# All of w_in decoded ahead of the mish part and parked in DRAM, GpSimd's sums on VectorE, the first token tile in the static order, one DMA a group

## The chip, the cores and the metric

The kernel runs on one core of a Trainium2 chip. The metric is the device time of one execution in microseconds (us). The trace is that of one profiled execution; its views count microseconds from the start of its span.

## What is computed

The reference chains three parts. Landmark attention on q, k and v of 4 batches, 8 heads, 576 positions and 64 columns a head gives x of 2304 tokens by 512. A gated MLP follows, and a mish MLP:

```python
def _moe_ref(x, w1, w2, w3, w_out) -> np.ndarray:
    a = x @ w1
    b = x @ w2
    h = a * b @ w3
    return (h @ w_out).astype(np.float32)
...
def _moe2_ref(x, w_in, w_out) -> np.ndarray:
    h = x @ w_in
    sp = np.where(h > 20.0, h, np.log1p(np.exp(np.minimum(h, 20.0))))
    g = h * np.tanh(sp)
    return (g @ w_out).astype(np.float32)
```

The mish MLP is 512 to 2048 to 512 wide, and is what the change is about. Its weights arrive as 64-bit words and are decoded to fp32 on the core.

## The kernel before, in words

Every product is made of three matmuls on split operands: `mm3` (L197 to L200) multiplies high by high, high by low and low by high part. "Hi" is a rounded copy (`copy`, on ScalarE L227, on GpSimd L229), "lo" what is left over (`less`, L232).

**Stages.** The attention and the weight products come first. Then, for each pair of batches, the products a and b (`xa`, `xb`), whose product `xm` goes to a tile `h`, and the y stage, which multiplies `h` with the combined weight W3: eight units u (half a batch each), of four blocks `y u m` of 24 matmuls each. A unit needs `h` split into hi and lo first: eight `sh u k` on ScalarE and eight `sl u k` on VectorE, into one of two `hs` buffers, so the split of unit u+1 waits until unit u-1 has been multiplied. The y stage of units 2 to 7 is the last before the mish part.

**The mish part.** It works on three token tiles of 768 tokens, and for each tile on eight groups (q = 0 to 7) of 256 columns of w_in: 24 groups g. A group's product with w_in is done by a seven-product scheme on 2x2 blocks: PE makes `Z0` to `Z6` (six matmuls of 384 columns each, lines L198 to L200 with `zw` or `hs` as weights) in two PSUM banks, and the banks are read between them. In order of a group: ScalarE copies bank 0 (`S`, L1310), VectorE makes `Q` (L1313), ScalarE mish (`E1`, two activations, L1272 and L1273), VectorE `R` (L1322), the sums `C22` and `C21` (L1332, L1333), mish `E2`, sum `C12` (L1339), mish `E3`, and the lo parts `L1`, `L2`, `L3` (L232). Z6 writes bank 0 again and must wait until C22 has read it; Z0 of the next group waits in the same way for C12, and Z4 for E1. Between them PE does the output products of the group before, in four parts `O0` to `O3` of nine matmuls of 512 columns (`o_part`). Group 0 has no such parts.

**What feeds it.** w_in and w_out of this part come in 32 units n of 512 KB (`x_ops`): load `ld n` on SP's queue into one of four raw buffers, `da` (ScalarE L210), `dm` (VectorE L216), `ds` (ScalarE L219), `db` (VectorE L223). w_in units go to `wf`, 512 columns at a time. For w_out unit f follow `wh f` (ScalarE), `wl f` (GpSimd, L232) and `ws f`, a store of the split unit to DRAM, as later tiles load it again. For each quad q of w_in columns GpSimd makes four sums `zs0` to `zs3` (L1037), seven `zh` (ScalarE) and seven `zl` (VectorE) split the operands into a `zw` buffer (two of them, 14 KB a partition), and `zd q` stores them to DRAM. Tokens are treated alike: four sums `yt` (GpSimd, L1037), seven `yh` and seven `yl` for each token tile.

**The order.** Each engine works its instructions off in the order in which the program issues them. Up to the y stage's end this is the list `ORDER`, written out token by token. In it stand the loads and decoding of units 0 to 3 and 8 to 11 (the first 1024 columns of w_in) and 4 to 7, quads 0 and 1, and the token operands of tile 0. For groups 0 to 7 a second list, `WITH`, says after which of the group's steps the rest is issued: units 12 to 31, quads 2 to 7. From group 6 on a `zw` buffer's seven parts of 256 KB are loaded from DRAM, each right behind the product that frees it (`after_z`, L1303), and two split w_out units of 512 KB a group (L1347). SP's queue carries all these loads and stores and is worked off in order too. In the last group of a tile the seven `yh` and `yl` of the next tile stand right behind the products that free their buffers.

Of the kernel before, what the change touches and what calls it, by code (L numbers as in the profile page):

```python
# [1396 lines left out]
```

## Time and profile before

| | us |
|---|---|
| median of 3 runs | 775.21 (774.81 to 776.62) |
| the profiled execution's own time | 775.96 |
| its span, first to last instruction | 774.18 |
| busy: PE, VectorE (DVE), ScalarE (ACT), GpSimd (POOL) | 739.4, 454.2, 346.0, 158.6 |

The span is what the trace covers; 1.78 us of the profiled execution's time lie outside it. Matmuls are pipelined, and a busy PE is not PE at its peak.

### The profile page before, as it was taken

How to read it: one execution, taken by the hardware profiler on the slowest of the kernel's cores; microseconds unless marked ns; L12 is line 12 of the kernel's file. 1: busy time of each engine (PE TensorE's matmuls, PEld its weight loads, DVE VectorE, ACT ScalarE, POOL GpSimd, SP SyncE). 2: the span in 40 equal slices, each digit the busy share in tenths (PEclk: the TensorE clock that was granted, in tenths of full speed). 3: DMA queues.
4: the chain of work that ended last, by engine and by line, in shares of the span. 5: the costliest groups of instructions: out<-in, count | busy, mean ns of one | idle time of the engine just before them, and what ended most of it. 6: DMA issues, size and time to landing. Idle time of an engine off the chain costs nothing.

```text
span 774.2 us, 13579 instructions
## 1 busy us (share of the span) xinstructions
PE 739.4 (96%) x5236; PEld 623.0 (80%) x5236; DVE 454.2 (59%) x870; ACT 346.0 (45%) x753; POOL 158.6 (20%) x176
## 2 busy tenths in 40 slices
...
GB/s 323 374 269 74 152 135 248 148 84 138 55 164 136 145 48 85 174 1 150 109 239 251 273 208 233 346 230 208 222 181 166 175 193 240 206 177 166 175 1 82
DMA packets 61440, 135.16 MB, mean 175 GB/s; under 512 B 5312, under 2 KB 22080, under 8 KB 60352
## 3 DMA queue, kind: packets, MB, share of 16 engines
...
q8 instruction: 41, 0.67, 0.4%
...
## 4 chain that ended last, share of the span: by engine, by line
PE 79%; DMA 7%; DVE 6%; ACT 4%; issue 2%; POOL 0%; SPq 0%; ACTq 0%; POOLq 0%; DVEq 0%
PE ps L198 23%; PE ps L200 23%; PE ps L199 23%; PE ps L363 4%; DMA raw<-in_w3T_dram 3%; DMA raw<-in_wo_dram 3%; PE ps L854 2%; DVE raw L216 2%; DMA raw<-in_w_dram 1%; PE ps L653 1%; DMA raw<-in_wi_dram 1%; ACT W L1273 1%; PE ps L457 1%; DVE yH L232 1%; ACT raw L219 1%
## 5 line engine op out<-in xcount | busy, mean ns | idle before, releaser
L198 PE MATMUL ps<-hs,W 128*128 128x288 f32 (+1 forms) x298 | 92.7, 311 | 0.0
L199 PE MATMUL ps<-hs,W 128*128 128x288 f32 (+1 forms) x298 | 92.1, 309 | 0.0
L200 PE MATMUL ps<-hs,W 128*128 128x288 f32 (+1 forms) x298 | 92.1, 309 | 0.0
L1272 ACT ACTIVATE hsb<-hsb 128x768 f32<-128x768 f32 (+1 forms) x48 | 32.9, 686 | 124.3 <-DVE hsb L1333 87.6
L216 DVE TENSOR_SCALAR raw<-raw 128x512 uint16<-128x512 uint16 x88 | 72.8, 862 | 24.7 <-ACT raw L210 24.4
L198 PE MATMUL ps<-AT,M 128*128 128x288 f32 x256 | 79.0, 309 | 1.7 <-ACT a L227 1.6
L199 PE MATMUL ps<-AT,M 128*128 128x288 f32 x256 | 75.5, 295 | 0.0
L200 PE MATMUL ps<-AT,M 128*128 128x288 f32 x256 | 75.5, 295 | 0.0
L363 PE MATMUL ps<-wo,raw 128*128 128x512 f32 x128 | 65.6, 639 | 7.8 <-DVE raw L223 5.9
L219 ACT ACTIVATE raw<-raw 128x512 f32<-128x512 f32 x88 | 58.7, 676 | 25.6 <-DVE raw L216 25.6
L210 ACT ACTIVATE raw<-raw 128x512 int32<-128x512 uint16 x72 | 48.3, 673 | 43.3 <-DMA raw<-in_w3T_dram 14.9
L198 PEld LDWEIGHTS ps<-hs,W 128*128 128x128 f32 x298 | 56.2, 188 | 3.0 <-issue 0.8
L200 PEld LDWEIGHTS ps<-hs,W 128*128 128x128 f32 x298 | 56.3, 189 | 1.7
L199 PEld LDWEIGHTS ps<-hs,W 128*128 128x128 f32 x298 | 56.5, 190 | 1.5
L198 PEld LDWEIGHTS ps<-AT,M 128*128 128x128 f32 x256 | 48.0, 188 | 11.5 <-ACT a L227 2.8
L232 DVE TENSOR_TENSOR W<-hsb,W 128x384 fp32r<-128x384 f32 (+1 forms) x72 | 53.4, 744 | 5.2 <-ACT W L1273 4.8
L363 PEld LDWEIGHTS ps<-wo,raw 128*128 128x128 f32 x128 | 23.6, 204 | 30.7 <-issue 17.2
L199 PEld LDWEIGHTS ps<-AT,M 128*128 128x128 f32 x256 | 48.1, 188 | 0.0
L200 PEld LDWEIGHTS ps<-AT,M 128*128 128x128 f32 x256 | 48.1, 188 | 0.0
L227 ACT ACTIVATE a<-ps 128x288 f32<-128x288 f32 x64 | 26.2, 411 | 39.3 <-PE ps L200 36.9
L1322 DVE TENSOR_TENSOR zt<-ps,zt 128x384 f32<-128x384 f32 x24 | 13.4, 559 | 51.5 <-PE ps L200 51.5
L892 DVE TENSOR_TENSOR h<-a,ps 128x288 f32<-128x288 f32 x64 | 28.4, 452 | 21.4 <-PE ps L200 18.0
...
## 6 DMA issues: line engine op xcount, KB each, us to landing
raw<-in_w_dram SPq DMA_DIRECT2D x64, 256.0 KB, 3.8
zw<-zd SPq DMA_DIRECT2D x56, 256.0 KB, 3.0
hs<-zd SPq DMA_DIRECT2D x56, 256.0 KB, 3.1
...
zd<-zw SPq DMA_DIRECT2D x4, 1792.0 KB, 6.6
zd<-hs SPq DMA_DIRECT2D x4, 1792.0 KB, 6.7
```

Of the source, the lines that this page charges most:

```text
L198: T.matmul(out=o, lhsT=lh, rhs=rh, start=first, stop=False, skip_group_check=partial)
L199: T.matmul(out=o, lhsT=lh, rhs=rl, start=False, stop=False, skip_group_check=partial)
L200: T.matmul(out=o, lhsT=ll, rhs=rh, start=False, stop=last, skip_group_check=partial)
L210: S.activation(w[..., 0], q[..., 1], ACTF.Copy, scale=2.0 ** -13, bias=2.0 ** -14 - 0.5)
L216: V.tensor_scalar(q[..., 1], q[..., 3], 0x8000, None, op0=ALU.bitwise_and)
L219: S.activation(f32(w[..., 1]), f32(w[..., 1]), ACTF.Copy, scale=2.0 ** -112)
L227: S.activation(o, x, ACTF.Copy)
L232: (G if e == "POOL" else V).tensor_tensor(o, x, f32(hi), op=ALU.subtract)
L363: T.matmul(out=got(f"acc{i}"), lhsT=f32(got(f"w3{n}")[:, o:o + 128, 0]), rhs=WO0[j // 4][:, j % 4], start=j == 0, stop=j == 7)
L854: T.matmul(out=got(f"p{c}{key}")[32 * i:32 * i + 32, 0:256], lhsT=LT[r, b, 2 * c + par, :], rhs=w12(f"w{bp}{s}{c}")[r, par * 256:par * 256 ...
L892: V.tensor_tensor(hslice(u, s), got("s" + key), got("b" + key)[:, 0:HALF], op=ALU.mult)
L1272: S.activation(e, src_, ACTF.Mish)
```

## The change

All eight units of columns 1024 to 2047 of w_in (16 to 19, 24 to 27) are decoded first, where units 0 to 3 and 8 to 11 stood, and stored to DRAM as decoded (`wfs 2`, `wfs 3`, 1 MB each); `wfl 2` and `wfl 3` load them when quads 4 and 6 come up. Units 0 to 3 and 8 to 11 move into the end of the ab stage and the y stage, units 12 to 15 and the beginning of 20 into the y stage. Four split w_out units that are ready before their place is free (`STAGED`: f = 1, 2, 3, 5) go to other tiles first, are stored from there, and come back by `wr f`. The sums `zs` and `yt` and the lo parts `wl` are made by VectorE. Groups 0 to 7 are now steps of `ORDER` like the rest; `WITH` is gone. From tile 1 on, one DMA of 1792 KB reloads a `zw` buffer at the end of a group (`reload`), and the next tile's `yt`, `yh`, `yl` stand behind `Q`, `L1`, `E2` and `L3`. The matmuls, the mish steps and their order on PE stay.

```diff
-WITH = (
-    "zs0 2,zs1 2,zs2 2,wh 2,wl 2,da 16|zh0 2,zl0 2,dm 16,ld 18,ws 2|zh1 2,zl1 2,ds 16,wh 3,wl 3,ld 19,ws 3,da 17|zh2 2,zl2 2,db 16,dm 17|zh3 2,zl3 2,zs3 2,ds 17,db 17,da 18,dm 18|zh4 2,zl4 2,zh5 2,zl5 2,zh6 2,zl6 2,zd 2",
...
-MADE = (0, 1, 2, 3, 8, 9, 10, 11, 4, 5, 6, 7, 16, 17, 18, 19, 12, 13, 14, 15, 24, 25, 26, 27, 20, 21, 22, 23, 28, 29, 30, 31)
+MADE = (16, 17, 18, 19, 24, 25, 26, 27, 0, 1, 2, 3, 8, 9, 10, 11, 4, 12, 5, 6, 7, 13, 14, 15, 20, 21, 22, 23, 28, 29, 30, 31)
+STAGED = {1: 0, 2: 1, 3: 2, 5: 3}
...
+    "ds 13,wh 2,db 13,y 7 0,wh 3,wr 1,wl 2,zh0 1,yl6 0,ws 2,ld 15,zh1 1,zh2 1,zh3 1,wl 3,zh4 1,zl0 1,zh5 1,ws 3,"
+    "wh 5,zl1 1,zl2 1,y 7 1,da 14,zl3 1,zl4 1,zl5 1,yh0 0,wl 5,ws 5,yl0 0,da 15,ld 20,y 7 2,zs3 1,dm 14,zh6 1,"
+    "dm 15,ye 7 1,ye 7 0,ye 6 3,zl6 1,ds 14,zd 1,zs0 2,wfl 2,ds 15,zs1 2,db 14,y 7 3,ye 7 2,yh2 0,zs2 2,ld 21,"
+    "da 20,yl2 0,db 15,wr 2,wr 3,dm 20,ye 7 3,wr 5,yt4 1,wh 6,Z0 0,ds 20,wl 6,S 0,Z1 0,db 20,ws 6,ld 22,zh0 2,"
+    "da 21,Q 0,Z2 0,zh1 2,yt1 1,E1 0,Z3 0,zl0 2,zh2 2,R 0,Z4 0,zh3 2,L1 0,Z5 0,C22 0,zh4 2,zl1 2,C21 0,Z6 0,zh5 2,"
+    "zl2 2,E2 0,C12 0,zl3 2,Z0 1,E3 0,L2 0,Z1 1,S 1,L3 0,da 22,Q 1,O0 0,dm 21,yt3 1,ds 21,zl4 2,Z2 1,zl5 2,zs3 2,"
...
+    def zw_all(g):
+        if g % 2:
+            return hs_a()[:, 0:3584]
+        if "zwa" not in LATE:
+            LATE["zwa"] = LATE["pw"].tile([128, 3584], F32R, tag="zw0", name="zw0")
+        return LATE["zwa"]
-        return (hs_a() if g % 2 else HS[2])[:, p * 512:(p + 1) * 512]
+        return zw_all(g)[:, p * 512:(p + 1) * 512]
...
+    def w_made(j):
+        if j == 2:
+            return HS[2][:, 0:2048].rearrange("p (k n) -> p k n", k=4)
+        return wf(j) if j < 2 else HS[3]
+    def w_flat(x):
+        return x.rearrange("p k n -> p (k n)")
+    def w_stage(f):
+        i = STAGED[f]
+        return late(f"W{i // 2}", 2048, f"wst{i // 2}")[:, i % 2 * 1024:(i % 2 + 1) * 1024]
...
-            return ops + [(f"db {n}", "DVE", lambda e: join(r(), wf(j)[:, i]))]
+            return ops + [(f"db {n}", "DVE", lambda e: join(r(), w_made(j)[:, i]))]
+        def to():
+            return w_stage(f) if f in STAGED else wo_slot(f)
         return ops + [
             (f"db {n}", "DVE", lambda e: join(r())),
-            (f"wh {f}", "ACT", lambda e: copy(e, wo_slot(f)[:, 0:512], f32(r()[..., 0]))),
-            (f"wl {f}", "POOL", lambda e: less(e, wo_slot(f)[:, 512:1024], f32(r()[..., 0]), wo_slot(f)[:, 0:512])),
-            (f"ws {f}", "SP", lambda e: nc.sync.dma_start(out=wod[f], in_=f32(wo_slot(f))))]
+            (f"wh {f}", "ACT", lambda e: copy(e, to()[:, 0:512], f32(r()[..., 0]))),
+            (f"wl {f}", "DVE", lambda e: less(e, to()[:, 512:1024], f32(r()[..., 0]), to()[:, 0:512])),
+            (f"ws {f}", "SP", lambda e: nc.sync.dma_start(out=wod[f], in_=f32(to())))]
+    def wo_load(u):
+        nc.sync.dma_start(out=f32(wo_slot(u)), in_=wod[u % (2 * NQ)])
...
-        return [(f"zs0 {q}", "POOL", f(0, a21, a22, ALU.add)),
...
+        return [(f"zs0 {q}", "DVE", f(0, a21, a22, ALU.add)),
+                (f"zs1 {q}", "DVE", f(1, 0, a11, ALU.subtract)),
+                (f"zs2 {q}", "DVE", f(a21, a11, a21, ALU.subtract)),
+                (f"zs3 {q}", "DVE", f(1, a12, 1, ALU.subtract))]
...
-        return [(f"yt4 {t}", "POOL", sub_(y_cuts(t, 0, 1), t_(0), b_(0, 1), b_(0, 0))),
...
+        return [(f"yt4 {t}", "DVE", sub_(y_cuts(t, 0, 1), t_(0), b_(0, 1), b_(0, 0))),
...
+                (f"yt5 {t}", "DVE", sub_(y_cuts(t, 0), t_(1), b_(1, 0), t_(1)))]
...
+    WFD = dr.tile([256, 2048], F32, name="wfd")
...
+    o_free = {0: done_ab, 1: ["y 6 3"], 2: [f"yl{p} 0" for p in range(7)], 3: [f"yl{p} 0" for p in range(7)],
+              4: done_ab, 5: all_y, 6: all_y}
+    def wo_free(f):
+        return o_free[f] if f < 7 else [f"O{p} {(f - 7) // 2}" for p in range(4)]
+    def made(s):
+        n = MADE[s]
         k, j, i = units[n]
+        f = 4 * j + i
         x = x_ops(n)
...
+        was = [last_read[MADE[s - 4]]] if s >= 4 else ["ld w171", f"db w1{6 + s // 2}{s % 2}"]
         step(x[0][0], "SP", was + ([f"ld {MADE[s - 1]}"] if s else []), x[0][2], {f"x {s}": "raw"} if s < 4 else {})
         early(x[1:5], [f"ld {n}"])
...
+        if k == 0:
+            steps[f"db {n}"][1].extend({0: ["wfs 3"], 1: all_m}.get(j, ["swap"]))
+            if i == 3 and j > 1:
+                step(f"wfs {j}", "SP", [f"db {m}" for m in MADE[s - 3:s + 1]],
+                     lambda e: nc.sync.dma_start(out=WFD[(j - 2) * 128:(j - 1) * 128, :], in_=w_flat(w_made(j))))
+            return
+        if f < 7:
+            placed(f)
+    def placed(f):
+        before = [f"db {8 * (f // 4) + 4 + f % 4}"] + wo_free(f)
+        if f in STAGED:
+            before = before[:1] + all_m
+        early(x_ops(8 * (f // 4) + 4 + f % 4)[5:], before)
+    def restore(f):
+        step(f"wr {f}", "SP", [f"ws {f}"] + wo_free(f), lambda e: wo_load(f))
+    def quad(q):
         ops = zs_ops(q)
...
+        free = {0: ["wfs 2"], 1: ["y 6 3"]}.get(q, [])
+        if q:
+            before = before + [f"zl{p} {q - 1}" for p in range(7)]
+        if q in (2, 3):
+            before = before + [f"db {n}" for n in range(8, 12)]
+        if q in (4, 6):
+            j = q // 2
+            step(f"wfl {j}", "SP", [f"wfs {j}"] + [f"zl{p} {x}" for x in (q - 4, q - 3) for p in range(7)],
+                 lambda e: nc.sync.dma_start(out=w_flat(wf(j)), in_=WFD[(j - 2) * 128:(j - 1) * 128, :]))
+        if q > 3:
+            before = before + [f"wfl {q // 2}"]
         early(ops[0:3], before)
         for p in range(6):
-            early(zp_ops(q, p), ["zs2 %d" % q] + free)
+            early(zp_ops(q, p), [f"zs2 {q}"] + free + ([f"Z{p} {q - 2}"] if q > 1 else []))
         early(ops[3:], [f"zl1 {q}", f"zl2 {q}", f"zs2 {q}"])
...
         early([z_store(q)], [f"zl{p} {q}" for p in range(7)])
...
+    def z_ops(g):
...
+        table = [
+            ("Z0", "PE", z_wait(0, f"C12 {p}", *all_y), lambda e: z_mm(g, 0)),
+            ("S", "ACT", [f"Z0 {g}", f"C21 {p}"], lambda e: S.activation(zt(0), b0, ACTF.Copy)),
+            ("Z1", "PE", z_wait(1, f"C21 {p}"), lambda e: z_mm(g, 1)),
+            ("Q", "DVE", [f"Z1 {g}", f"S {g}", f"C12 {p}"], lambda e: add(zt(1), b1, zt(0)))]
+        o = [(f"O{i}", "PE", o_wait(i), lambda e, i=i: o_part(p, i)) for i in range(4)] if g else []
+        table += o[0:1] + [
...
+        return [(f"{n} {p if n[0] == 'O' else g}", e, w, fn) for n, e, w, fn in table]
...
+    for s in range(MADE.index(20)):
+        made(s)
...
+    quad(0)
+    quad(1)
+    for f in STAGED:
+        restore(f)
+    nt = next_tile(1)
+    for g in range(NQ):
+        for name, e, w, fn in z_ops(g):
+            step(name, e, w + (chain("pe", name) if e == "PE" else []), fn)
+        for f in range(7, 2 * NQ):
+            if (f - 5) // 2 == g:
+                placed(f)
+        for n in {0: (20, 21, 22), 1: (23, 28), 2: (29, 30), 3: (31,)}.get(g, ()):
+            made(MADE.index(n))
+        if g + 2 < NQ:
+            quad(g + 2)
...
+    def reload(g):
+        if NQ <= g + 2 < NG:
+            nc.sync.dma_start(out=f32(zw_all(g)), in_=zd[(g + 2) % NQ])
+        for u in (2 * g + 5, 2 * g + 6):
+            if 2 * NQ <= u < 2 * NG:
+                wo_load(u)
+    for g in range(5, NQ):
+        reload(g)
+    for g in range(NQ, NG):
+        t, q = divmod(g, NQ)
+        more = {}
+        if t < 2 and q > 4:
+            x = next_tile(t + 1)[q]
+            cuts = {5: (0, 0, 0, 2), 6: (0, 1, 1, 1), 7: (5, 9, 11, 15)}[q]
+            more = dict(zip(("Q", "L1", "E2", "L3"), (x[i:j] for i, j in zip((0, *cuts), cuts))))
+        for name, e, _, fn in z_ops(g):
             fn(e)
...
-        def after_z(p):
-            if g + 2 < NG and g + 2 >= NQ:
-                nc.sync.dma_start(out=f32(zw_slot(g + 2, p)), in_=zd[(g + 2) % NQ][:, p * 512:(p + 1) * 512])
...
+            for _, e, fn in more.get(name.split()[0], ()):
+                fn(e)
+        reload(g)
```

## Rows read from the trace of the kernel before

**Rows 1.** The page: busy time of each engine.

```profile
PE 739.4 (96%) x5236; PEld 623.0 (80%) x5236; DVE 454.2 (59%) x870; ACT 346.0 (45%) x753; POOL 158.6 (20%) x176
```

**Rows 2.** Busy time by stretch: five engines, granted clock, DMA share, GB/s.

```profile
302.20:368.80 66.60, 66.60 (x506) 66.60 (x505) 39.41 (x64) 33.34 (x85) 22.21 (x20) 1.00 0.26 96
368.80:384.10 15.30, 8.35 (x44) 7.20 (x42) 8.83 (x16) 9.77 (x19) 3.48 (x3) 0.87 0.45 138
438.70:457.60 18.90, 15.93 (x80) 14.01 (x79) 15.28 (x22) 10.65 (x22) 10.64 (x9) 1.00 0.78 262
482.00:498.00 16.00, 16.00 (x81) 14.39 (x80) 8.70 (x15) 9.16 (x16) 3.98 (x3) 1.00 1.01 369
```

**Rows 3.** Timeline, ScalarE: start and length of each group's S.

```profile
370.05 0.49 ACT L1310 ACTIVATE zt<-ps 128x384 f32<-128x384 f32 x1 [0.66 <-PE ps L200]
...
386.42 0.49 ACT L1310 ACTIVATE zt<-ps 128x384 f32<-128x384 f32 x1 [0.48 <-PE ps L200]
...
420.21 0.47 ACT L1310 ACTIVATE zt<-ps 128x384 f32<-128x384 f32 x1
...
440.92 0.48 ACT L1310 ACTIVATE zt<-ps 128x384 f32<-128x384 f32 x1
...
510.24 0.49 ACT L1310 ACTIVATE zt<-ps 128x384 f32<-128x384 f32 x1 [0.43 <-PE ps L200]
...
620.12 0.49 ACT L1310 ACTIVATE zt<-ps 128x384 f32<-128x384 f32 x1 [1.61 <-PE ps L200]
...
637.65 0.49 ACT L1310 ACTIVATE zt<-ps 128x384 f32<-128x384 f32 x1 [0.45 <-PE ps L200]
...
747.53 0.49 ACT L1310 ACTIVATE zt<-ps 128x384 f32<-128x384 f32 x1 [1.62 <-PE ps L200]
```

**Rows 4.** Timeline, PE, group 0: idle time before in brackets.

```profile
374.20 0.44 PE L198 MATMUL ps<-yH,zw 128*128 128x384 f32 x1 [1.04 <-ACT W L1273]
...
379.43 0.44 PE L198 MATMUL ps<-ym,zw 128*128 128x384 f32 x1 [2.88 <-DVE hsb L1332]
...
384.10 0.69 PE L198 MATMUL ps<-yW,hs 128*128 128x384 f32 x1 [3.04 <-DVE hsb L1339]
```

**Rows 5.** Timeline, ScalarE and VectorE, group 0.

```profile
371.98 1.28 ACT L1272 ACT_TABLE_LOAD   x1
...
377.14 1.21 DVE L223 SCALAR_TENSOR_TENSOR wf<-raw 128x512 int32<-128x512 int32 x1
...
378.79 0.58 DVE L1332 TENSOR_TENSOR hsb<-ps,zt 128x384 f32<-128x384 f32 x1
```

**Rows 6.** Timeline, ScalarE in group 3, VectorE in group 4.

```profile
432.05 0.67 ACT L210 ACTIVATE raw<-raw 128x512 int32<-128x512 uint16 x1 [4.85 <-DMA raw<-in_wi_dram]
...
452.95 1.95 DVE L232 TENSOR_TENSOR zw<-wf,zw 128x256 fp32r<-128x256 f32 x1 [2.01 <-ACT zw L227]
454.82 2.33 DVE L216 TENSOR_SCALAR raw<-raw 128x512 uint16<-128x512 uint16 x1
456.95 0.57 DVE L1339 TENSOR_TENSOR hsb<-ps,zt 128x384 f32<-128x384 f32 x1
```

**Rows 7.** Instructions of two tiles and two lines, ns.

```profile
L232 DVE TENSOR_TENSOR zw<-wf,zw x16: 411/774/1945, 312.5 to 460.2; 128x256 fp32r<-128x256 f32 x16
...
L216 DVE TENSOR_SCALAR raw<-raw x88: 723/750/2330, 5.6 to 488.5; 128x512 uint16<-128x512 uint16 x88
...
L223 DVE SCALAR_TENSOR_TENSOR wf<-raw x16: 681/688/1206, 255.6 to 441.1; 128x512 int32<-128x512 int32 x16
...
L232 DVE TENSOR_TENSOR yH<-sums,yH x9: 945/957/959, 328.7 to 630.4; 128x768 fp32r<-128x768 f32 x9
```

**Rows 8.** Timeline, VectorE, last group of tile 1.

```profile
629.31 2.06 DVE L232 TENSOR_TENSOR yH<-sums,yH 128x768 fp32r<-128x768 f32 x2 [0.86 <-ACT yH L227]
```

**Rows 9.** The page: DMA issues, KB each, us to landing.

```profile
zw<-zd SPq DMA_DIRECT2D x56, 256.0 KB, 3.0
...
zd<-hs SPq DMA_DIRECT2D x4, 1792.0 KB, 6.7
```

More of the change, by code (lines that the diff above doesn't have):

```diff
@@ L909, in swap @@
         HS.extend(pw.tile([128, 8 * 2 * HALF], F32R, tag=f"hs{i}", name=f"hs{i}") for i in range(2))
-        HS.append(pw.tile([128, 7 * 512], F32R, name="zw0"))
+        HS.append(pw.tile([128, 7 * 512], F32, tag="zw0", name="wst"))
         HS.append(pw.tile([128, 4, 512], F32, name="wf0"))
@@ L1061, in f @@
         def f(e):
-            x = (hs_a() if q % 2 else HS[2])[:, 0:3584]
-            nc.sync.dma_start(out=zd[q], in_=f32(x))
+            nc.sync.dma_start(out=zd[q], in_=f32(zw_all(q)))
         return (f"zd {q}", "SP", f)
@@ L1176 @@
-    for s, n in enumerate(MADE[:12]):
+    all_y = [f"y 7 {m}" for m in range(4)]
+    last_read = {n: f"db {n}" if units[n][0] == 0 else f"wl {4 * units[n][1] + units[n][2]}" for n in MADE}
+    o_free = {0: done_ab, 1: ["y 6 3"], 2: [f"yl{p} 0" for p in range(7)], 3: [f"yl{p} 0" for p in range(7)],
[4 more added lines that the diff above has]
+        n = MADE[s]
         k, j, i = units[n]
+        f = 4 * j + i
@@ L1178 @@
         x = x_ops(n)
-        n_ = MADE[s - 4]
-        was = ["ld w171", f"db w1{6 + s // 2}{s % 2}"] if s < 4 else [f"db {n_}"]
+        was = [last_read[MADE[s - 4]]] if s >= 4 else ["ld w171", f"db w1{6 + s // 2}{s % 2}"]
         step(x[0][0], "SP", was + ([f"ld {MADE[s - 1]}"] if s else []), x[0][2], {f"x {s}": "raw"} if s < 4 else {})
         early(x[1:5], [f"ld {n}"])
-        steps[f"db {n}"][1].extend(all_m if j == 1 else ["swap"])
-    for f in range(2):
-        early(x_ops(4 + f)[5:], [f"db {4 + f}"] + (done_ab if f == 0 else ["y 6 3"]))
@@ L1186 @@
-    for n in MADE[12:14]:
-        early(x_ops(n)[:1], [f"wl {MADE[MADE.index(n) - 4] - 4}"])
-    for q in range(2):
-        free = ["swap"] if q == 0 else ["y 6 3"]
-        ops = zs_ops(q)
-        before = [f"db {n}" for n in range(4)] + hs_read[0] + ([f"zl{p} 0" for p in range(7)] if q else [])
+        if k == 0:
[4 more added lines that the diff above has]
+            return
@@ new lines, in made @@
+        if f < 7:
[8 more added lines that the diff above has]
+    def quad(q):
+        ops = zs_ops(q)
+        before = [f"db {n}" for n in range(4)] + hs_read[0]
+        free = {0: ["wfs 2"], 1: ["y 6 3"]}.get(q, [])
[9 more added lines that the diff above has]
+            before = before + [f"wfl {q // 2}"]
@@ L1202, with zt @@
-    ones = sbt([128, 512], "ones", 1, BF16)
-    V.memset(ones, 1.0)
-    for _ in range(SPIN):
-        T.matmul(out=bank[7], lhsT=ones[:, 0:128], rhs=ones, start=True, stop=True)
-    issue()
     z_bank = bank[0:2]
     o_bank = bank[2:8]
-    ZT = late("A", 3 * QT, "zt", F32)
-    s_, q_, r_ = (ZT[:, i * QT:(i + 1) * QT] for i in range(3))
+    def zt(i):
+        return late("A", 3 * QT, "zt", F32)[:, i * QT:(i + 1) * QT]
     def c_of(i):
@@ L1222, in g_of, with z_mm @@
         return w3_flat(g % 2)[:, o:o + TT]
-    def z_mm(g, p, x, first):
+    def z_mm(g, p):
+        x = (0, 1, 0, 1, 0, 1, 0)[p]
         for c in range(2):
             mm3(z_bank[x][:, 0:QT], zw(g, p, 0)[:, c], zw(g, p, 1)[:, c], y_op(p, 0)[:, c], y_op(p, 1)[:, c],
-                first and c == 0, c == 1 and p in (2, 5, 6), True)
+                p in (0, 1, 4) and c == 0, c == 1, True)
     begun, oc = set(), [0]
@@ L1233, in o_mm @@
         c, w = slice(i * 128, (i + 1) * 128), wo_slot(2 * g + e)
-        key = (t, i)
-        n = sum(1 for k in begun if k[:2] == key)
-        begun.add((*key, n))
+        n = sum(1 for k in begun if k[:2] == (t, i))
+        begun.add((t, i, n))
         mm3(o_bank[i], g_of(g, e, 0)[:, c], g_of(g, e, 1)[:, c], w[:, 0:512], w[:, 512:1024], n == 0, n == 2 * NQ - 1)
@@ L1257, in o_part @@
     def o_part(g, part):
-        if g < 0:
-            return
         t, q = divmod(g, NQ)
```

147 lines of the change are left out of this document (62 added, 85 removed), and 86 rows, old and new, of tables (ORDER, WITH).

## Prediction

> **What bounds the kernel now.** I read the page first, then busy time by stretch, then the timeline of the mish part. TensorE (PE) is busy for 739.4 of 774.2 us; VectorE, ScalarE and GpSimd have more than 300 us free each [rows 1]. So time can come only out of PE's idle time or its lower clock, and the stretches say where that is. In the y stage from 302.2 to 368.8 us PE never stops: 506 matmuls in 66.6 us, 0.132 us for one of 288 columns. There is nothing to win there, only to lose. In group 0 it is busy for 8.35 of 15.3 us at a mean granted clock of 0.87 (full is 2.4 GHz, the lower level 1.2), in group 4 for 15.93 of 18.9 [rows 2].
>
> The starts of `S` give the groups' lengths [rows 3]. From 637.65 to 747.53 seven groups take 109.88 us, 15.70 each: PE without a gap. Group 0 takes 16.37 us though it has no output products. Groups 1 to 7 take 510.24 - 386.42 = 123.82 us, 13.9 more than seven times 15.70; group 3 alone (420.21 to 440.92) has 5.0 of it. The last group of tile 1 takes 17.53 us, 1.83 too much.
>
> The causes differ. In group 0 PE waits 1.04 us for mish, 2.88 for `C22`, 3.04 for `C12` [rows 4]. C22's input is ready about 1 us after 374.20, yet it runs at 378.79, behind decoding that was issued ahead of it [rows 5]: head-of-line blocking on VectorE. In group 3 ScalarE sat 4.85 us in front of a `da` whose load had not landed. In group 4 a `zl` took 1.95 us and a `dm` 2.33, and C12 came out behind them at 456.95 [rows 6]; the same forms can take 0.411 and 0.723 us [rows 7]. GpSimd was busy for 10.64 us of this stretch [rows 2].
>
> **Group 0 after the change.** Only `L1` stands between R and C22 on VectorE, and no quad or unit ahead of C12 that waits for a load. Up to Z4 I keep 374.2 us, as S, the table load of 1.28 us [rows 5] and E1 stay. Six matmuls of 384 columns take 6 x 0.132 x 384/288 = 1.06 us (estimate from rows 2). Z4 ends at 375.3, C22 (0.58 us, rows 5) at 375.9, Z5 at 376.3, Z6 at 377.4, C12 at 378.0. Z0 of group 1 starts at 378.1 and S about 1.3 us later, at 379.4 instead of 386.42: **7.0 us**.
>
> **Groups 1 to 7.** With twelve units less to decode here, with steps that VectorE and ScalarE reach in time and with PE's clock up, each takes 15.70 us: **13.9 us**. VectorE has room: in a group as full as the fourth stand 2 `dm`, 3 `db`, 4 `zs`, 7 `zl`, 2 `wl` and the group's own eight. With 0.75 and 0.69, and 0.41 for each of 256 columns [rows 7], 0.68 for 512 and 0.55 for 384 (estimates between 0.411 at 256 and 0.957 at 768), this is 1.5 + 2.1 + 1.6 + 2.9 + 1.4, and five sums of 0.58, two of 0.55 and one of 0.957 make 5.0: 14.4 of 15.70 us. That is full, but instructions overlap: the dm of 454.82 ends at 457.15, the next starts at 456.95 [rows 6].
>
> **Tile ends.** In the last group of tile 1 two `yl` hold VectorE for 2.06 us up to 631.4 [rows 8], just where C22 is due. Moved behind L1, E2 and L3 they have slack: **1.8 us** (bounds 0 and 1.83). For tile 0 it is in the 13.9.
>
> **One DMA a group.** It waits for Z6 of its group; two groups on, Z0 needs it. Between lie one output part of nine matmuls (2.1 us by 0.132 x 512/288) and a whole group, 17.8 us; 256 KB land in 3.0 us, and the nearest row of 1792 KB, a store, took 6.7 [rows 9]. Nothing gained or lost: the work of the group between hides it, and PE would wait only if it landed more than 17.8 us after its issue. Behind it in SP's queue stand two w_out loads needed a group later still.
>
> **The y stage.** Here the work goes that left the mish part, with no PE gap to pay for it. On VectorE `dm` goes from 4 to 15, `db` from 4 to 14, `zs` from none to 11, `yt` to 5, `wl` to 6: 11 x 0.75 + 10 x 0.69 + 11 x 0.41 + 5 x 0.957 + 6 x 0.68 = 28.6 us on top of 39.4 [rows 2, 7]. That makes 68.0 of 66.6 us if nothing else changes. But GpSimd's 22.2 us there [rows 2] are mostly these sums and go: 14 `zl` at 0.411 instead of the median 0.774 give back 5.1, and 43 added instructions that overlap by 0.1 to 0.2 give 4 to 9. I take 55 to 59. ScalarE gets 26 more of about 0.67 us [rows 6], 17.4 on 33.3. What counts is when the splits `sl` of the next unit end. They may start when the unit before begins (12.7 us each) and stand first in the list; for units 6 and 7 they are mixed with decoding up to the second and third block, 6.3 us in, and have six left. I take 0.5 us lost, bounds 0 and 3. The ab stage holds two units and two stores of 1 MB more, on engines with room: nothing.
>
> **DMA at the seam.** During unit 7 these are issued: ten transfers of 512 KB (`ws` 2, 3, 5, `ld` 15, 20, 21, `wr` 1, 2, 3, 5), `zd 1` of 1792 KB and `wfl 2` of 1 MB, 8.1 MB. The most that a stretch shows is 369 GB/s at a share of 1.01 [rows 2]: 22 us, in 12.7. `ld 21` has 6.0 MB ahead of it; with its own 0.5 that is 17.8 us from 356.1, landing at 373.9. `da 21` stands ahead of E1 on ScalarE and could run at 371.0 (S ends at 370.5 [rows 3], one copy stands between). So E1 and Z4 come some 3 us late; bounds 0 (the load overtakes) and 7 (the three `wr` share the engines, 378.1). **I take 3.** The Trainium skill ("DMA: Bandwidth & Descriptors", section "Where 436 GB/s comes from") puts the ceiling at 436 GB/s. By it the load would land at 371.1 plus its fixed part of some 2 us and cost 2 us instead of 3; no run here shows that rate.
>
> Other loads of groups 1 to 5 follow `zd` and `ws` on the same queue; one late load cost group 3 its 5.0 us [rows 3, 6]. **I take 2 us**, bounds 0 and 5.
>
> **The sum.** 7.0 + 13.9 + 1.8 = 22.7 won, 0.5 + 3 + 2 = 5.5 given back: 17.2. The span falls from 774.18 to 757.0, the profiled execution's time from 775.96 to 758.8. The median of the runs is 0.75 below that execution: **758.0 us**.
>
> **Rivals.**
> A. Late loads still set the first tile. For: the backlog above, and rows 6. Then da 21 costs 7 us and half of the 13.9 stays: 22.7 - 7 - 7 - 0.5 = 8.2 won, 767.0. Against: w_in's loads are gone from it. Chance 0.15.
> B. VectorE becomes the bound in the y stage, and the kernel slower. For: 68.0 against 66.6 us, and an in-order queue in which decoding stands between splits. If units 4 to 7 each get their splits 6 us late, PE loses 24 us more: 782. It decides where the splits end more than 12.7 us after their unit may start; below that nothing is lost. Against: they come first, and GpSimd's collisions are gone. Chance 0.07. A rule of the Trainium skill speaks for it ("Perfetto Trace Analysis", "Optimizing Scalar/DVE Operations"): a saturated VectorE should hand work to ScalarE or even GpSimd, the reverse of this edit. It adds that the two share an SBUF read port, so that moving between them might not help; rows 6 and 7 bear that out, which is why I give B little.
> C. All waits vanish: 22.7 won, 752.5. For: the bounds of 0 above. Chance 0.15.
> D. The moved work frees group 0 but the static order stalls as often elsewhere, or the edits don't reach PE at all: 773 to 777. Against: rows 4 to 6 name waits whose cause is taken away. Chance 0.05.
>
> **How the numbers follow.** The forecast, 753.5 to 766, has 0.58. The range 751.5 to 769 takes in C, the forecast and most of A, and leaves out some 0.15. A measurement of this kernel tells 0.3%, 2.3 us, from no change. Faster: 0.58 + 0.15 + 0.15 = 0.88; same: D's 0.05; slower: B's 0.07.
>
> **What would show it.** Right: S of group 1 about 9 to 12 us behind S of group 0, later groups near 15.7, the last group of tile 1 too; `zl` at 0.41 us throughout; GpSimd empty from the y stage on; PE still without a gap there. ScalarE idle ahead of `da 21` on a load shows the 3 us. Wrong: PE idle in the y stage behind `sl` (B), VectorE in use for over 95% of groups 1 to 4, ScalarE waiting for loads in several groups (A), or PE waiting for a 1792 KB load in tile 1 or 2.

## Result: 9 us faster, about half of what was forecast

The median of the changed kernel is 765.92 us (765.49 to 769.49, 4 runs) against 775.01 (774.31 to 776.62, 4 runs) of the kernel before, a ratio of 0.989 with a 95% interval of 0.9856 to 0.9924. The forecast was 758.0 with a range of 751.5 to 769. Between the two profiled executions the span fell by 10.5 us, 774.18 to 763.7, where 17.2 were forecast; the medians differ by 9.1, as neither profiled execution is the median one.

The page of the kernel after, busy time by engine, beside [rows 1]:

```profile
PE 739.3 (97%) x5236; PEld 625.5 (82%) x5236; DVE 456.7 (60%) x935; ACT 347.1 (45%) x753; POOL 81.6 (11%) x111
```

PE is busy as long as before; GpSimd has lost half of its time, VectorE's sum has hardly moved. The time must again be looked for by stage. The copies `S` (now L1347) on the timeline of ScalarE, beside [rows 3] (start, duration in us):

```profile
369.93 0.47 ACT L1347 ACTIVATE zt<-ps 128x384 f32<-128x384 f32 x1
...
385.85 0.49 ACT L1347 ACTIVATE zt<-ps 128x384 f32<-128x384 f32 x1
...
401.56 0.49 ACT L1347 ACTIVATE zt<-ps 128x384 f32<-128x384 f32 x1 [0.44 <-PE ps L214]
...
438.86 0.49 ACT L1347 ACTIVATE zt<-ps 128x384 f32<-128x384 f32 x1 [0.36 <-PE ps L214]
...
501.75 0.49 ACT L1347 ACTIVATE zt<-ps 128x384 f32<-128x384 f32 x1 [0.88 <-PE ps L214]
...
611.63 0.49 ACT L1347 ACTIVATE zt<-ps 128x384 f32<-128x384 f32 x1 [1.62 <-PE ps L214]
...
627.81 0.47 ACT L1347 ACTIVATE zt<-ps 128x384 f32<-128x384 f32 x1
...
642.98 0.49 ACT L1347 ACTIVATE zt<-ps 128x384 f32<-128x384 f32 x1 [0.90 <-PE ps L214]
```

Group 0 takes 15.92 us (16.37 before; 9.4 forecast, 12.4 with the 3 us given back for a late load). Groups 1 to 7 take 501.75 - 385.85 = 115.90 (123.82 before; 111.9 forecast, with the 2 us given back): group 1 15.71, groups 2 and 3 together 37.30, 5.9 more than 31.40, groups 4 to 7 15.72 each. The last group of tile 1 takes 16.18 and the next 15.17, 31.35 together (33.17 before), so the 1.8 us came. Group 0 gave 0.45 us, groups 1 to 7 7.92 and the tile end 1.82; with some 0.3 elsewhere that is the 10.5. All that is missing lies in groups 0, 2 and 3, 3.5 us and 4.0.

What ended the waits there: the timelines of ScalarE and of PE after (a bracket is the idle time before the instruction and its releaser):

```profile
375.30 0.65 ACT L224 ACTIVATE raw<-raw 128x512 int32<-128x512 uint16 x1 [4.59 <-DMA raw<-in_wo_dram]
...
419.46 0.67 ACT L224 ACTIVATE raw<-raw 128x512 int32<-128x512 uint16 x1 [5.81 <-DMA raw<-in_wo_dram]
...
378.49 0.69 PE L212 MATMUL ps<-yH,zw 128*128 128x384 f32 x1 [5.35 <-ACT W L1325]
...
379.30 0.52 PE L214 MATMUL ps<-yH,zw 128*128 128x384 f32 x1
379.62 0.52 PE L212 MATMUL ps<-yH,zw 128*128 128x384 f32 x1
...
382.73 0.34 PE L213 MATMUL ps<-yH,zw 128*128 128x384 f32 x1
382.90 0.34 PE L214 MATMUL ps<-ym,zw 128*128 128x384 f32 x1
...
422.24 0.45 PE L212 MATMUL ps<-yW,hs 128*128 128x384 f32 x1 [1.95 <-ACT zt L1347]
...
424.22 0.69 PE L212 MATMUL ps<-yH,hs 128*128 128x384 f32 x1 [0.66 <-DVE zt L1328]
```

`da 21` (375.30) waited 4.59 us for its load; the table load and mish of group 0 stand behind it, and PE waited 5.35 us for that mish. `da 28` (419.46) waited 5.81 us; behind it came mish of group 2 and `S` of group 3, and PE waited 1.95 us for `S` and 0.66 for `Q`, which stood behind a `db`, a `dm` and a sum on VectorE that had waited too. The timeline of SP's queue shows what was issued ahead of the two loads:

```profile
364.74 0.32 SPq L1101 DMA_DIRECT2D zd<-hs  x1
365.10 0.43 SPq L1252 DMA_DIRECT2D wf<-wfd  x1
365.58 0.91 SPq L1043 DMA_DIRECT2D raw<-in_wo_dram  x1
...
404.70 1.46 SPq L1101 DMA_DIRECT2D zd<-hs  x1
406.21 0.42 SPq L1252 DMA_DIRECT2D wf<-wfd  x1
406.73 1.18 SPq L1063 DMA_DIRECT2D wod<-hs  x1
407.96 1.25 SPq L1043 DMA_DIRECT2D raw<-in_wo_dram  x1
```

The chain of work that ended last has both loads (start, us to landing):

```profile
365.58 9.70 DMA raw<-in_wo_dram
...
407.96 11.42 DMA raw<-in_wo_dram
```

`ld 21` was issued at 365.58, behind `zd 1` and `wfl 2`, and took 9.70 us to land. These three are 3.4 MB (1.84, 1.05 and 0.52). In the 10.5 us from the first issue to that landing, 364.74 to 375.28, the DMA engines moved 379 GB/s, which is 4.0 MB, so some 0.6 MB of other transfers went with them. `ld 28` stood behind `zd 3`, `wfl 3` and a `ws` and took 11.42.

The windows after, beside [rows 2]: us, busy us and instructions of PE, PEld, DVE, ACT, POOL, granted clock, DMA share, GB/s:

```profile
302.20:368.60 66.40, 66.40 (x503) 66.40 (x502) 52.66 (x108) 47.73 (x111) 0.00 (x0) 1.00 0.55 201
355.60:368.60 13.00, 13.00 (x99) 13.00 (x98) 10.95 (x23) 9.24 (x22) 0.00 (x0) 1.00 0.93 346
356.10:375.28 19.18, 16.77 (x115) 15.80 (x114) 15.36 (x30) 10.64 (x24) 0.00 (x0) 1.00 0.97 359
364.74:375.28 10.54, 8.13 (x50) 7.16 (x48) 8.18 (x14) 5.23 (x11) 0.00 (x0) 1.00 0.98 379
...
375.80:382.60 6.80, 4.11 (x13) 4.11 (x14) 1.45 (x3) 3.81 (x9) 0.00 (x0) 0.50 0.87 307
423.60:430.40 6.80, 6.18 (x16) 5.31 (x17) 5.65 (x14) 2.64 (x7) 0.00 (x0) 0.50 1.01 361
```

In the y stage PE has no gap, with VectorE at 52.66 and ScalarE at 47.73 us and GpSimd empty. From 375.80, within the first wait, to 382.60 and from 423.60, within the second, to 430.40 the granted clock is 0.50, the level of 1.2 GHz. A matmul of 384 columns starts 0.32 us behind the one before it there (379.30, 379.62), and some 0.176 at full clock (382.73, 382.90).

Operations on VectorE are short again. All `zl` into `zw` between 360 and 500 us (minimum, median, maximum in ns), beside [rows 7]:

```profile
L246 DVE TENSOR_TENSOR zw<-wf,zw x12: 405/419/455, 372.5 to 450.2; 128x256 fp32r<-128x256 f32 x12
```

### The profile page after: what moved, and what is told of

Read it like the earlier page. It is cut to its first block, busy times and chain, and to the rows that moved or that the text cites. A ratio compares the mean times of both kernels' runs of the same rounds, so it can differ in the third digit from the quotient of the medians.

```text
span 763.7 us, 13273 instructions
## 1 busy us (share of the span) xinstructions
PE 739.3 (97%) x5236; PEld 625.5 (82%) x5236; DVE 456.7 (60%) x935; ACT 347.1 (45%) x753; POOL 81.6 (11%) x111
## 4 chain that ended last, share of the span: by engine, by line
PE 85%; DMA 8%; DVE 3%; ACT 2%; issue 1%; SPq 0%; ACTq 0%
PE ps L212 25%; PE ps L214 24%; PE ps L213 24%; DMA raw<-in_wo_dram 6%; PE ps L377 5%; PE ps L868 2%; PE ps L471 2%; PE ps L667 1%; DMA raw<-in_w_dram 1%; DMA raw<-in_w3T_dram 1%; DVE raw L237 1%; PE ps L549 1%; PE ps L587 1%; PE ps L608 1%; DVE raw L230 1%
## 5 line engine op out<-in xcount | busy, mean ns | idle before, releaser
L1328 DVE TENSOR_TENSOR hsb<-ps,zt 128x384 f32<-128x384 f32 x72 | 40.2, 558 | 95.5 <-PE ps L214 95.5
L1328 DVE TENSOR_TENSOR zt<-ps,zt 128x384 f32<-128x384 f32 x48 | 26.8, 557 | 87.1 <-PE ps L214 83.1
L230 DVE TENSOR_SCALAR raw<-raw 128x512 uint16<-128x512 uint16 x88 | 64.8, 773 | 18.1 <-ACT raw L224 17.7
L377 PE MATMUL ps<-wo,raw 128*128 128x512 f32 x128 | 63.4, 622 | 7.9 <-DVE raw L237 6.8
L246 DVE TENSOR_TENSOR W<-hsb,W 128x384 fp32r<-128x384 f32 (+1 forms) x72 | 49.2, 685 | 15.2 <-ACT W L1325 15.0
L377 PEld LDWEIGHTS ps<-wo,raw 128*128 128x128 f32 x128 | 23.0, 198 | 28.6 <-issue 15.5
```

The costliest lines, as they stand in the source:

```text
L230: V.tensor_scalar(q[..., 1], q[..., 3], 0x8000, None, op0=ALU.bitwise_and)
L246: (G if e == "POOL" else V).tensor_tensor(o, x, f32(hi), op=ALU.subtract)
L377: T.matmul(out=got(f"acc{i}"), lhsT=f32(got(f"w3{n}")[:, o:o + 128, 0]), rhs=WO0[j // 4][:, j % 4], start=j == 0, stop=j == 7)
L1328: V.tensor_tensor(o, x, y, op=ALU.add)
```

## The experiments

In all edits of the list only the order of tokens changes; the engines work them off as listed. All times are medians; a span is that of the profiled execution. The kernel before was measured again beside each set: 774.82 us beside experiments 1 to 4, 775.68 beside 5 to 8, 775.50 beside 9, so medians of different sets are compared only to some 0.9 us. Profiled executions also differ ahead of the y stage, which the edits of experiments 1 to 7 don't touch: it starts between 300.26 us (experiment 4) and 304.50 (experiment 2). So a stage is read by its own length.

**1. The first late load alone.** One token is moved.

```diff
-...da 15,ld 20,y 7 2,...,zd 1,zs0 2,wfl 2,...,zs2 2,ld 21,da 20,...
+...da 15,ld 20,ld 21,y 7 2,...,zd 1,zs0 2,wfl 2,...,zs2 2,da 20,...
```

> The load of unit 21 is issued right behind that of unit 20, ahead of zd 1 and wfl 2. Theory (bytes ahead in SP's queue make it late): it lands in 3 to 6 us, before 368, ScalarE no longer waits ahead of da 21, group 0 takes 9.2 to 10 us from S to S instead of 15.92, PE's clock stays up there, and the kernel comes to 759 to 760. Rival (VectorE and ScalarE are too full at the seam, the load is only the last to arrive): group 0 stays within 1.5 us of 15.9 and the time at 764.5 to 766.

759.62 us (759.0 to 760.57), ratio to before 0.9799 (0.9782 to 0.9815). Group 0 takes 9.36 us (371.69 to 381.05). The waits of ScalarE for loads moved on but hit only one place (timeline of ScalarE):

```profile
415.07 0.65 ACT L221 ACTIVATE raw<-raw 128x512 int32<-128x512 uint16 x1 [6.20 <-DMA raw<-in_wo_dram]
```

This is `da 28`, and group 2 takes 20.54 us. Ahead of it ScalarE waits 4.47 us in group 1, which has slack, as it is full of output products: it takes 15.72 us.

**2. The second late load alone.**

```diff
-...ws 7,ld 23,zd 3,zs0 4,wfl 3,wl 8,...,da 23,ld 28,zl2 4,...
+...ws 7,ld 23,zs0 4,wl 8,...,da 23,ld 28,zd 3,wfl 3,zl2 4,...
```

> zd 3 and wfl 3 are issued behind the load of unit 28 instead of ahead of it. Theory: 2.9 MB less stand ahead of it, it lands some 8 us earlier, groups 2 and 3 take 31.4 to 33 us together instead of 37.3, and the kernel comes to 760 to 762. Rival (the wait only moves on: unit 29 now stands behind zd 3 and wfl 3 as well, and ScalarE waited 5.2 us for it already): groups 2 to 4 together stay within 2 us of 53.1 and the time at 764 to 766.

761.36 us (759.74 to 764.1), ratio 0.9827 (0.9804 to 0.985). Group 0 takes 16.10 us again, groups 2 and 3 15.65 and 16.95.

**3. Both.**

> Both moves together. Theory: the two waits are separate and add: group 0 9.2 to 10 us, groups 1 to 7 near 15.7 each, 753.5 to 755.5. Rival: what is won at one place is lost at the next load, 758 to 761.

753.9 us (752.77 to 755.66), ratio 0.973 (0.9713 to 0.9746), span 751.0, faster than either kernel. The copies `S` of groups 0, 1, 3, 4 and 8 (L1344 here), and the windows of two stretches, the first around group 0, the second over parts of groups 2 and 3 (columns as above):

```profile
369.35 0.48 ACT L1344 ACTIVATE zt<-ps 128x384 f32<-128x384 f32 x1
...
378.71 0.49 ACT L1344 ACTIVATE zt<-ps 128x384 f32<-128x384 f32 x1
...
410.07 0.49 ACT L1344 ACTIVATE zt<-ps 128x384 f32<-128x384 f32 x1 [0.37 <-PE ps L211]
...
426.24 0.47 ACT L1344 ACTIVATE zt<-ps 128x384 f32<-128x384 f32 x1
...
489.07 0.49 ACT L1344 ACTIVATE zt<-ps 128x384 f32<-128x384 f32 x1 [0.88 <-PE ps L211]
```

```profile
368.60:384.40 15.80, 14.43 (x75) 12.72 (x75) 13.12 (x26) 11.23 (x23) 0.00 (x0) 1.00 0.75 282
...
400.10:415.80 15.70, 15.70 (x80) 14.13 (x79) 12.23 (x28) 9.84 (x22) 0.00 (x0) 1.00 1.00 403
```

Group 0 takes 9.36 us, and the granted clock is 1.00 throughout. The same decoding, sums and transfers run; only two loads of 512 KB go ahead of stores and loads of 1 to 1.8 MB. ScalarE still waits for four loads in groups 1 to 4, 2.0 to 4.0 us each; at most the 0.5 us by which group 3 is too long (426.24 - 410.07 = 16.17) come of it.

**4. The first load later still.**

```diff
-...,zs2 2,ld 21,da 20,yl2 0,db 15,wr 2,wr 3,dm 20,ye 7 3,wr 5,yt4 1,...
+...,zs2 2,da 20,yl2 0,db 15,wr 2,wr 3,dm 20,ye 7 3,wr 5,ld 21,yt4 1,...
```

> The load of unit 21 is issued behind wr 2, wr 3 and wr 5, three more transfers of 512 KB. Theory: 1.57 MB at the 346 to 369 GB/s that this stretch moves are 4.3 to 4.5 us; da 21 starts at 379.6 to 380 instead of 375.3, group 0 takes 20 to 20.5 us and the kernel 769.5 to 770.5. Rival (VectorE and ScalarE set group 0): nothing changes, 765 to 766.

769.58 us (one run). ScalarE sits idle ahead of `da 21` twice as long, and group 0 takes 20.46 us, 4.5 more than in the changed kernel:

```profile
378.95 0.65 ACT L222 ACTIVATE raw<-raw 128x512 int32<-128x512 uint16 x1 [9.41 <-DMA raw<-in_wo_dram]
```

So the price follows the load's place in the queue in both directions.

**5. GpSimd's sums back.** On the kernel of experiment 3.

```diff
-            (f"wl {f}", "DVE", ...
+            (f"wl {f}", "POOL", ...
-        return [(f"zs0 {q}", "DVE", ...      (zs0 to zs3, yt4, yt1, yt3, yt5)
+        return [(f"zs0 {q}", "POOL", ...
```

> Kernel: the one with both loads early (753.9 us, a span of 751.0), with the engine of zs, yt and wl set back to GpSimd; the order stays. Theory: GpSimd's sums and VectorE's operations stretch each other, as the rows of before show for zl (0.411 to 1.945 us). Then zl and dm go up to 0.7 us and more wherever GpSimd is busy, the sums themselves take 0.9 instead of 0.42 us, C12 and C22 come late again in groups 0 to 5, PE waits for them, and the time is 757 to 763. Rival: the moved decoding alone emptied the first tile, and VectorE, which is rid of some 28 us of sums, only gains room: no PE wait, 753 to 755.5.

757.31 us (756.91 to 760.06), ratio 0.9776 (0.9747 to 0.9804): 3.4 us slower than experiment 3 (2.5 when each is set against the kernel before of its own set), at the edge of what the theory gave, but in another place. Groups 1 to 4 take 15.70, 15.65, 16.18 and 16.20 us; the loss sits ahead of the first `S`. The timelines of VectorE, ScalarE and PE there:

```profile
368.39 2.56 DVE L243 TENSOR_TENSOR yW<-y,yW 128x768 fp32r<-128x768 f32 x1 [0.67 <-ACT yW L238]
370.87 1.78 DVE L234 SCALAR_TENSOR_TENSOR raw<-raw 128x512 int32<-128x512 int32 x1
372.57 2.33 DVE L227 TENSOR_SCALAR raw<-raw 128x512 uint16<-128x512 uint16 x1
...
374.94 0.67 ACT L230 ACTIVATE raw<-raw 128x512 f32<-128x512 f32 x1 [4.58 <-DVE raw L227]
375.50 0.47 ACT L1344 ACTIVATE zt<-ps 128x384 f32<-128x384 f32 x1
...
376.03 0.69 PE L209 MATMUL ps<-yW,zw 128*128 128x384 f32 x1 [4.86 <-ACT zt L1344]
```

GpSimd is busy from 366.4 to 376.4 us with a pause of 0.3. Under it a `yl` takes 2.56 us (0.957 in [rows 7]), a `db` 1.78 and `dm 20` 2.33. `ds 20` waits for that `dm` on ScalarE, `S` stands behind `ds 20`, and PE waits 4.86 us for `S`. This execution is the slowest of the four (760.06), so the median holds less of that wait. The transfers are not what stretches VectorE: in experiment 3 the same `yl` and `dm` take 0.96 and 0.78 us with GpSimd empty, at a DMA share of 1.01 from 364 to 374 us; here the share is 1.01 too, from 366.4 to 376.4. With twelve units less to decode there, groups 1 to 4 bear GpSimd's sums with little loss.

**6. Seven reloads of 256 KB.** On the kernel of experiment 3, groups 8 on.

```diff
+            if name[0] == "Z" and g + 2 < NG:
+                p = int(name[1])
+                nc.sync.dma_start(out=f32(zw_slot(g, p)), in_=zd[(g + 2) % NQ][:, p * 512:(p + 1) * 512])
```

> Kernel: both loads early, but from group 8 on a zw buffer is loaded as in the kernel before, by seven DMAs of 256 KB a group, each right behind the product that frees it. Theory (the prediction's term of nothing): the loads have a whole group of slack either way, groups stay at 15.70 us, the time is 753.9 within 0.8. Rival: the 98 DMAs more hold up SP's queue or the w_out loads behind them: PE waits in tiles 1 and 2, 755.5 or more.

754.34 us (753.09 to 755.96), 0.44 from experiment 3, less than the sets differ by. From 633.67 to 727.91 six groups take 94.24 us, 15.71 each. One DMA a group neither gains nor loses.

**7. The old end of tile 1.** On the kernel of experiment 3.

```diff
-        if t < 2 and q > 4:
+        if t == 0 and q > 4 or t == 1 and q in (5, 6):
...
+            if t == 1 and q == 7 and name[0] == "Z":
+                p = int(name[1])
+                for _, e, fn in yp_ops(2, p) + (ysum_ops(2)[3:] if p == 1 else []):
+                    fn(e)
```

> Kernel: both loads early, but in the last group of tile 1 the seven yh and yl of the next tile stand behind their products again, as in the kernel before; the end of tile 0 stays as it is. Theory: the last group of tile 1 takes 17.5 instead of 15.7 us, since two yl hold VectorE while C22 is due: 755.3 to 756.0. Rival: what made that group long before was GpSimd's yt beside the yl (VectorE makes the yt now): 15.7 to 16.2 us, 753.9 to 754.5.

756.72 us (756.12 to 757.31), ratio 0.976 (0.9735 to 0.9786), above the 755.3 to 756.0 expected. The last group of tile 1 takes 618.64 - 601.23 = 17.41 us, and the pair of `yl` of [rows 8] is back (timelines of ScalarE and VectorE):

```profile
584.74 0.49 ACT L1344 ACTIVATE zt<-ps 128x384 f32<-128x384 f32 x1 [1.61 <-PE ps L211]
...
601.23 0.47 ACT L1344 ACTIVATE zt<-ps 128x384 f32<-128x384 f32 x1
...
618.64 0.49 ACT L1344 ACTIVATE zt<-ps 128x384 f32<-128x384 f32 x1 [0.43 <-PE ps L211]
...
634.28 0.49 ACT L1344 ACTIVATE zt<-ps 128x384 f32<-128x384 f32 x1 [0.90 <-PE ps L211]
...
610.38 2.00 DVE L243 TENSOR_TENSOR yH<-sums,yH 128x768 fp32r<-128x768 f32 x2 [1.25 <-ACT yH L238]
```

It and the next group take 33.05 us together, 1.7 more than the 31.35 of the changed kernel. The group before counts too: the last group's `S` comes late, behind a `yh` on ScalarE, so that the group before shows 16.49 us. The three groups take 634.28 - 584.74 = 49.54 us, against 47.05 (583.25 to 630.30) in experiment 3: the old end costs 2.5 us, of which PE waits 1.7. GpSimd is empty there. The other 0.3 of the 2.8 us between the medians are less than the sets differ by.

**8. VectorE's cover in the y stage.** On the kernel of experiment 3, each `dm` of the 16 units that are decoded there, or just ahead, runs twice.

```diff
-(f"dm {n}", "DVE", lambda e: sign(r()))
+(f"dm {n}", "DVE", lambda e: [sign(r()) for _ in range(1 + (n in TWICE))])
+TWICE = (0, 1, 2, 3, 8, 9, 10, 11, 4, 12, 5, 6, 7, 13, 14, 15)
```

> Kernel: both loads early, and every dm of the 16 units that are decoded from the end of the ab stage through the y stage is made twice (the second writes the same values): about 11 us more work on VectorE in the y stage, some 63 instead of 52.8 us busy of 66.4. Theory (splits stand first in the list, cover is left): PE loses 0 to 3 us there, 753.9 to 757. Rival (the prediction's B: an in-order VectorE has no cover left, splits of units 4 to 7 each come late): PE idle behind sl, 6 us or more a unit, 765 to 778.

758.89 us, but wide, 755.14 to 761.19; ratio 0.9784 (0.9747 to 0.982). The profiled execution (span 755.7) in the y stage:

```profile
302.20:368.60 66.40, 66.40 (x504) 66.40 (x504) 60.08 (x117) 45.53 (x106) 0.00 (x0) 1.00 0.54 191
```

VectorE is busy for 60.08 of 66.40 us and PE has no gap. Behind it `ds 20` waits 0.96 us for `dm 20`, PE waits 0.60 us for a copy and 1.26 for `S`, and `S` to `S` of group 0 takes 9.64 us. The median lies outside both forecasts, nearer to the theory's 757 than to the rival's 765, and the time is not lost behind `sl`. Of the 4.7 us between this span and that of experiment 3, 1.1 lie ahead of the y stage (it starts at 302.17 us, and at 301.05 in experiment 3), 2.2 between the first `Z0` and its `S` (3.88 us, 1.64 in experiment 3) and 1.3 in groups 0, 3 and 4. So with the `dm` doubled the loss sits at the seam and behind it.

**9. GpSimd's sums to VectorE, in the kernel before.** The edit of experiment 5, the other way round and alone.

> Kernel: the one before, with a single part of the change: zs, yt and wl made by VectorE; all decoding, its order and the lists stay. Theory (two causes, and the order of decoding is the larger): zl goes back to 0.41 us, dm to 0.75 and the sums to 0.42, but decoding still stands ahead of C22 and C12 and the late loads stay, and VectorE has some 28 us of sums more; group 0 stays at 15 to 16.5 us, groups 1 to 7 lose 6 to 13 us instead of 13.9; time 767 to 774. Rival 1 (GpSimd's collisions were the main cause): groups 1 to 7 come to 15.7 to 16.2 us each, 760 to 765. Rival 2 (VectorE too full in the first tile): they lose 15 us or more, 776 to 782.

771.49 us (770.77 to 771.73), ratio 0.9951 (0.9934 to 0.9967). `zl` is short, but the groups are not (all `zl` into `zw` from 360 to 500 us, and `S` of groups 1 and 8 on the timeline of ScalarE):

```profile
L232 DVE TENSOR_TENSOR zw<-wf,zw x12: 417/422/455, 372.1 to 454.7; 128x256 fp32r<-128x256 f32 x12
```

```profile
384.63 0.49 ACT L1310 ACTIVATE zt<-ps 128x384 f32<-128x384 f32 x1 [0.49 <-PE ps L200]
...
505.82 0.49 ACT L1310 ACTIVATE zt<-ps 128x384 f32<-128x384 f32 x1 [0.43 <-PE ps L200]
```

Group 0 takes 15.80 us, groups 1 to 7 505.82 - 384.63 = 121.19, still 11.3 more than 109.9. So of the 13.9 us some 2.6 went with the collisions, net of the work that VectorE took over. Group 3 alone takes 20.29 us (417.04 to 437.33); there a load of w_in is late (timeline of ScalarE):

```profile
428.37 0.66 ACT L210 ACTIVATE raw<-raw 128x512 int32<-128x512 uint16 x1 [4.95 <-DMA raw<-in_wi_dram]
```

So the 11.3 that stay hold the place of the decoding and that of its loads. They are gone in experiment 3, where both are moved; no run here parts the two.

## Where the prediction held and where it fell short

- **Group 0, 7.0 won.** Right: without the late load it takes 9.36, forecast 9.4, and C22 no longer stands behind decoding. That it is right to 0.04 us is luck: in experiment 3 Z4 starts 3.91 us behind `S` (4.15 taken), and the steps from Z4 to the next `S` take 5.45 us (5.2 taken).
- **DMA at the seam, 3 lost.** The right place, the right instruction (`da 21`), too small a size: 15.92 - 9.36 = 6.56 us, inside the bounds of 0 and 7. The load landed at 375.3, not 373.9 (6.9 MB had moved since 356.1, at 359 GB/s; 6.5 MB at 369 were taken), and ScalarE idled 4.59 us. PE's wait ahead of Z4 rose from 0.7 us (experiment 3) to 5.35, 4.65 of the 6.56. The other 1.9 are the 1.2 GHz stretch behind the wait: some 13 matmuls of 384 columns at 0.32 instead of 0.176 us each. The prediction counted a wait and left out the clock that follows it. Experiments 1 and 4 show the term's size by its cause: 6.3 us back when the load goes first, 3.7 us more when it goes last (one run). An estimate by the Trainium skill's ceiling ("DMA: Bandwidth & Descriptors", "Where 436 GB/s comes from") would have made the term 2, with the load landing at 373.1; the trace does not bear that out. The same section of the Trainium skill gives some 436 GB/s as the fabric's ceiling and says that some 358 GB/s bind transfers between HBM and SBUF, which these are. Here the 359 GB/s up to the landing are near that; but from 364.74 on it was 379, and a stretch of experiment 3 (400.10 to 415.80) moved 403 at a share of 1.00, so stretches of this case lie above it.
- **Other loads, 2 lost.** 5.9 us, past the upper bound of 5. One load did nearly all of it, `ld 28`: groups 2 and 3 take 31.82 us together in experiment 3, 5.5 less than 37.30. PE's waits in groups 2 and 3 are 1.95 + 0.66 = 2.6 us; the other 3.3 us are mostly the second stretch at 0.50. Experiment 2 gave 4.6 us back between the medians.
- **Groups 1 to 7, 13.9 won.** Right once `ld 28` is early: in experiment 3 they take 489.07 - 378.71 = 110.36 us, 0.46 over seven times 15.70. Experiment 9 splits its cause: the place of the decoding and its loads is the larger part (11.3), GpSimd's collisions the smaller (2.6). Both were in the argument, unweighted.
- **Tile ends, 1.8 won.** Right, 1.82; experiment 7, which puts the old end into the new order, cost 2.5.
- **One DMA a group, nothing.** Right. The median landing is 7.3 us, within the 17.8 of slack:

```profile
zw<-zd SPq DMA_DIRECT2D x8, 1792.0 KB, 7.3
```

- **The y stage, 0.5 lost.** No gap. VectorE was expected at 55 to 59 us and has 52.66 (the added work there comes to 28.5 us, not 28.6, which changes nothing); ScalarE at 50.7 and has 47.73. Rival B did not come, and at 60.08 us busy (experiment 8) there is still no gap.
- **The rivals.** A's mechanism, late loads that set the first tile, is what happened in groups 0, 2 and 3. A priced them at 7 and at half of 13.9, that is 7; 6.56 and 5.9 came. Its 767.0 is 1.1 us from the 765.92 measured, the forecast's 758.0 is 7.9, and the measured time lies 0.08 inside the forecast's upper end. Of the two cases the less likely one was the better account; against it stood that w_in's loads are gone from the first tile, but both loads that were late are of w_out. C's 752.5 is near what the kernel comes to once both go early (753.9). The rule of the Trainium skill cited for B ("Perfetto Trace Analysis", "Optimizing Scalar/DVE Operations") names the port that the two engines share as a reason why moving between them might not help. The runs agree that the two disturb each other (2.33 us for `dm 20` beside GpSimd, a median of 0.75 in [rows 7]); that the port is the reason no run shows. Yet taking the sums off GpSimd helped, by 4.0 us in experiment 9 and by 2.5 to 3.4 in experiment 5.

The step that failed is the size of the two terms for late loads: 3 and 2 us were forecast, 6.56 and 5.9 measured, 12.5 together (12.0 between the medians of the changed kernel and of experiment 3). One part of the error is common to both: a wait of PE was priced by its length alone, and the stretch at 1.2 GHz behind each wait cost 1.9 us and most of 3.3 more. The other part is the landing: 1.4 us later than taken for `ld 21`, and 11.42 us behind a `zd`, a `wfl` and a `ws` for `ld 28`, whose place in the queue the prediction did not work out.
